# The first attention rounds of a fused sparse-attention and mixture-of-experts kernel: another order of their steps, unread matmuls beside them

## The chip, the core and the metric

The kernel runs on one core of a Trainium2 chip. The metric is device time in microseconds, the median of three runs. Five engines work side by side and wait for one another by semaphores: TensorE (PE: matmuls; PEld: its weight loads), VectorE (DVE), ScalarE (ACT), GpSimd (POOL) and SyncE (SP), which here issues the DMAs. Each engine takes its instructions in program order.

## The reference

Attention over 4 batches, 8 heads, 576 positions and 64 channels: heads 0 to 3 see the last 32 positions (local), heads 4 to 7 every 32nd position (strided). Its output, laid out as 2304 rows of 512, goes through 8 experts with a Sinkhorn gate.

```python
scores = scale * np.matmul(q, k.transpose(0, 1, 3, 2))
scores = np.where(masks[None], scores, -1e9)
attn = np.exp(scores - scores.max(-1, keepdims=True))
attn = attn / (attn.sum(-1, keepdims=True) + 1e-9)
x = np.matmul(attn, v).transpose(0, 2, 1, 3).reshape(2304, 512)
P = np.exp(x @ w_gate - max)          # then 8 x: rows to 1, columns to N / E
for e in range(8):
    out += P[:, e:e + 1] * (np.maximum(x @ w1[e], 0) @ w2[e])
```

## The kernel before

**Numbers.** To keep fp32 precision at the speed of the one-pass type, an operand is split into a high part (rounded, by ACT) and a low part (the rest, by DVE or POOL); a product is then three matmuls. This holds for x, the hidden layer h and the expert weights. Scores, transposes and values use plain fp32.

**Attention steps.** There are 32 steps k, eight for each batch: a pair of heads and half of the positions. In the order of `STEPS`, steps 0 to 3 of a batch are strided (0 and 2 with two blocks of 126 positions for each head, 1 and 3 with three blocks of 108), 4 to 7 local (4 and 5 with four windows, 6 and 7 with five). One step passes through all the engines:

- `at_scores`: PE multiplies queries and keys (tiles `sc`, L223 or L240), DVE scales and masks each window into `sm` and takes its extreme (L253), ACT takes the exponential and its sum (L259).
- `at_normalize`: DVE inverts the sums (L268, L269), POOL multiplies `sm` by them (L271).
- `at_transpose`: PE transposes `sm` into `tp` (L283), DVE copies it to `pt` (L284).
- `at_values`: PE multiplies with the values into `pv` (L296 or L310); ACT writes the high part of x into `reg` (L329), DVE the low part (L330). A strided step of the first batch does this in two pieces, and the second piece of ACT waits for the first of DVE.

`load_qkv(k)` issues two DMAs on SP: queries with keys (`qk`, three buffers) and values (`v`, five buffers). A load into a used buffer waits on SP until the matmuls that read it are done, and everything behind it on SP waits too.

**Weights.** Expert 0 is computed without a Strassen scheme, while attention is still running. Its weight tiles come in the order of the list `plain` by `load_w` into four slots of `raws`; `split_w` splits one (ACT L180, POOL L181) and issues the load of the next, which waits for POOL to have freed a slot. Before, `plain` alternates w1 and w2 tiles.

**Rounds.** Nine rounds k = 0 to 8 open the program, with LAG = 3: scores of k, values of k - 3, loads of k + 2, transposes of k - 2, normalization of k - 1, then one weight tile is split. Rounds 6 to 8 also begin the first layer of expert 0 (`begin_layer1`, L410: three matmuls for a weight tile ft and a quarter dt of the 512 channels; x of quarter dt must be there). Eight of the 16 pieces (ft, dt) are begun there, dt 2 and 3; the first four calls of `layer1` add dt 0 and 1.

**Slots.** Then come 56 slots. A slot has one call of `layer1` (tile `ph`, L424: 12 matmuls; h by ACT L430 and DVE L431) and the call of `layer2` of the slot before (tile `y`, L448: 6 matmuls). The first 26 also carry attention: layer1, values of k - 3, scores of k, layer2, transposes of k - 2, normalization of k - 1. After them the gate, the Strassen operands and the experts 1 to 7 follow; nothing of that changes.

PSUM tiles: tag s (scores), t (transposes; `pv` in the slots), y (`pv` in the rounds; `y`), l1 (`ph`), two buffers each.

Of the kernel before, what the change touches and what calls it, by code (L numbers as in the profile page):

```python
# [55 lines left out]
def kernel(  # L56
# [97 lines left out]
    plain = [(u, ft, which) for u in range(UPE) for ft in range(FH) for which in range(2)]  # L154
    plain[2 * FH :] = sorted(plain[2 * FH :], key=lambda x: (x[0], x[1] + 1.5 * x[2]))
# [43 lines left out]
    qkv_t, sms, sums_t, pts = {}, {}, {}, {}  # L199
# [87 lines left out]
    def at_values(k, tag):  # L287
# [40 lines left out]
        for src, (hi, lo) in moves:  # L328
            nc.scalar.activation(hi, src, AF.Copy)  # L329
            nc.vector.tensor_tensor(lo, src, hi.bitcast(F32), op=ALU.subtract)  # L330
# [84 lines left out]
    def layer1(u, c, ft):  # L415
        c0, n = c
        if u == 0 and c0 == 0:
            ph, dts = begun[ft // 2][:, ft % 2, :], (0, 1)
        else:
            ph, dts = ps.tile([P, 4 * P], F32, tag="l1", name=f"ph_{u}_{c0}_{ft}"), range(NDT)  # L420
        w = wt[u, ft, 0]
        for dt in dts:
            for i, x in ((0, 0), (0, 1), (1, 0)):
                nc.tensor.matmul(  # L424
                    ph[:, :n], w[:, i, dt, :], xv(x, dt, c0, n),
                    start=(dt + i + x == 0 and len(dts) == NDT),
                    stop=(dt == dts[-1] and i == 1), skip_group_check=len(dts) < NDT,
                )
        h = pools["h"].tile([P, 2, 4 * P], F32R, tag="h", name=f"h_{u}_{c0}_{ft}")
        nc.scalar.activation(h[:, 0, :n], ph[:, :n], AF.Relu)  # L430
        nc.vector.scalar_tensor_tensor(  # L431
            h[:, 1, :n], ph[:, :n], 0.0, h[:, 0, :n].bitcast(F32), op0=ALU.max, op1=ALU.subtract
        )
        hs[u, c0, ft] = h
# [553 lines left out]
    LAG = 3  # L988
    at_k = 0

    def attention_scores():
        if at_k < NS:
            at_scores(at_k)

    def attention_rest():


        nonlocal at_k
        if 0 <= at_k - 2 < NS:
            at_transpose(at_k - 2)  # L1000
        if 0 <= at_k - 1 < NS:
            at_normalize(at_k - 1)
        at_k += 1

    def attention_values(tag="t"):
        if at_k:
            store_x()
        if 0 <= at_k - LAG < NS:
            at_values(at_k - LAG, tag)
        if at_k:  # L1010
            load_qkv(at_k + 2)

    load_qkv(0)
    nc.sync.dma_start(cst, consts)
    load_qkv(1)
    load_qkv(2)
    for _ in range(4):
        load_w()
    nc.sync.dma_start(wg_raw, wg.rearrange("(k p) e -> p k e", p=P))
    nc.gpsimd.memset(ones, 1.0)  # L1020
    nc.gpsimd.memset(wgs.bitcast(F32), 0.0)
    for k in range(2 * NP - 2 + LAG):
        attention_scores()
        attention_values("y")
        attention_rest()
        if 1 <= k <= 2 * FH:
            split_w(*plain[k - 1])
        for x in {6: ((0, 2), (1, 2)), 7: ((2, 2), (0, 3)), 8: ((1, 3), (2, 3), (3, 2), (3, 3))}.get(k, ()):
            begin_layer1(*x)
    for dt in range(NDT):  # L1030
        c = 2 * E * dt
        nc.scalar.activation(wgs[:, c : c + E], wg_raw[:, dt, :], AF.Copy)
        nc.vector.tensor_tensor(
            wgs[:, c + E : c + 2 * E], wg_raw[:, dt, :], wgs[:, c : c + E].bitcast(F32),
            op=ALU.subtract,
        )
# [55 lines left out]
    for slot, (u, c, ft, last) in enumerate(slots):  # L1092
# [3 lines left out]
        busy = at_k < NS + LAG  # L1096
        if busy:
            attention_values()
# [8 lines left out]
        if busy:  # L1107
            attention_rest()
# [129 lines left out]
```

## Time and profile before

| | us |
|---|---|
| median of three runs | 1571.06 (1570.34 to 1572.72) |
| the profiled execution | 1571.07 |
| its span, first to last instruction | 1569.2 |
| PE busy in the span | 1550.7 (99%) |
| DVE, POOL, ACT busy | 1270.9, 972.0, 538.4 |
| HBM traffic | 413.82 MB, 264 GB/s |

A busy PE is not a PE at its peak: matmuls are pipelined and their ends are modelled. To see what bounds a stretch, the chain of waits is read: it goes back from the last instruction, at each step to what released it, or to the instruction before it on its engine. PE holds 94% of it.

### The profile page before, as it was taken

The numbers are of one execution on the slowest core, as the hardware profiler recorded it, in microseconds if no ns is written. First come the engines' busy times: TensorE is split into PE (matmuls) and PEld (weight loads), VectorE is DVE, ScalarE is ACT, GpSimd is POOL, SyncE is SP. The second block draws the span as 40 slices with busy tenths as digits, with TensorE's granted clock in tenths as the row PEclk, the third lists the DMA queues.
The fourth block names the chain that finished last, engine by engine and source line by source line (L and its number), as shares of the span: only waits on it lengthen the run. The fifth ranks groups of instructions, "written<-read, shape, count | busy, mean of one in ns | idle before, by whom it ended". The sixth has DMA issues, their size and how long they took to land.

```text
span 1569.2 us, 25435 instructions
## 1 busy us (share of the span) xinstructions
PE 1550.7 (99%) x9146; PEld 1455.8 (93%) x9146; DVE 1270.9 (81%) x2457; ACT 538.4 (34%) x1261; POOL 972.0 (62%) x899
## 2 busy tenths in 40 slices
PE   7999999999999999999999999999999999999999
PEld 5888887889999989898999999999999999999998
DVE  4665256689999999997688888888868888888887
ACT  6665222333434434342423322222232322222221
POOL 4222357265556565561777777877867777777874
PEclk9999999999999999999999999999999999999999
DMA  6553558897988888887967766766757666666762
GB/s 206 197 168 115 181 203 294 283 334 279 364 309 335 308 334 312 319 315 278 353 254 288 281 234 256 292 236 250 282 214 294 272 259 268 273 243 256 281 235 94
DMA packets 116622, 413.82 MB, mean 264 GB/s; under 512 B 9264, under 2 KB 63120, under 8 KB 102544
## 3 DMA queue, kind: packets, MB, share of 16 engines
q1 hardware_dynamic: 116496, 412.19, 69.7%
q8 instruction: 73, 1.20, 0.3%
q14 instruction: 53, 0.43, 0.1%
HBM read 275.27 MB, written 136.89 MB: 263 GB/s over the span
## 4 chain that ended last, share of the span: by engine, by line
PE 94%; DMA 2%; DVE 2%; POOL 1%; ACT 1%; issue 0%; SPq 0%; POOLq 0%; DVEq 0%; ACTq 0%
PE p L818 25%; PE bb L688 16%; PE yg L717 16%; PE bc L688 11%; PE ba L688 11%; PE y L448 6%; PE ph L424 5%; PE tp L283 1%; DMA rb<-in_w 1%; PE pv L296 1%; PE sc L223 1%; PE sc L240 1%; PE pv L310 1%; DMA qk<-in_qkv 1%; PE pl L339 1%; DMA sx<-xd 1%
## 5 line engine op out<-in xcount | busy, mean ns | idle before, releaser
L826 DVE TENSOR_TENSOR total<-p,total 128x384 f32<-128x384 f32 x714 | 371.9, 557 | 0.8 <-PE p L818 0.8
L688 PE MATMUL bb<-reg 128*128 128x384 f32 x1512 | 304.3, 335 | 1.1 <-DVE u L741 0.7
L688 PEld LDWEIGHTS bb<-reg 128*128 128x128 f32 x1512 | 266.0, 188 | 4.1 <-DVE u L741 1.0
L688 PE MATMUL bc<-reg 128*128 128x384 f32 x1008 | 201.9, 334 | 0.5 <-ACT h L749 0.5
L688 PE MATMUL ba<-reg 128*128 128x384 f32 x1008 | 201.8, 334 | 0.0
L799 ACT ACTIVATE a<-u 128x384 fp32r<-128x384 f32 x106 | 55.7, 525 | 359.3 <-DVE u L793 359.1
L741 DVE TENSOR_TENSOR u<-bb,m 128x384 f32<-128x384 f32 x168 | 93.3, 555 | 104.8 <-PE bb L688 101.5
L688 PEld LDWEIGHTS bc<-reg 128*128 128x128 f32 x1008 | 177.3, 188 | 0.8 <-ACT h L749 0.8
L688 PEld LDWEIGHTS ba<-reg 128*128 128x128 f32 x1008 | 177.3, 188 | 0.1
L875 POOL TENSOR_TENSOR s1t<-m,u 128x384 f32<-128x384 f32 x53 | 53.9, 1016 | 188.3 <-DVE m L793 188.3
L724 DVE SCALAR_TENSOR_TENSOR acc<-yg,gate,acc 128x512 f32<-128x512 f32 x186 | 131.4, 741 | 9.6 <-PE yg L717 9.6
L717 PE MATMUL yg<-w2b,h 128*128 128x512 f32 x504 | 117.4, 390 | 0.4 <-DVE acc L724 0.4
L717 PE MATMUL yg<-w2t,h 128*128 128x512 f32 x504 | 117.1, 390 | 0.0
L818 PE MATMUL p<-s,w2b 128*128 128x384 f32 x648 | 116.7, 334 | 0.0
L717 PEld LDWEIGHTS yg<-w2b,h 128*128 128x128 f32 x504 | 94.3, 188 | 20.0 <-DVE acc L724 0.9
L448 PE MATMUL y<-w2t,h 128*128 128x512 f32 x432 | 111.4, 399 | 1.3 <-DVE acc L461 0.9
L818 PEld LDWEIGHTS p<-s,w2b 128*128 128x128 f32 x648 | 112.7, 188 | 0.0
L818 PE MATMUL p<-s,w2t 128*128 128x384 f32 x624 | 112.3, 334 | 0.0
L717 PEld LDWEIGHTS yg<-w2t,h 128*128 128x128 f32 x504 | 94.4, 188 | 19.1
L424 PE MATMUL ph<-reg,w 128*128 128x256 f32 (+1 forms) x648 | 110.4, 319 | 0.0
L803 POOL TENSOR_TENSOR a<-u,a 128x384 fp32r<-128x384 f32 x106 | 109.4, 1032 | 0.0
L818 PEld LDWEIGHTS p<-s,w2t 128*128 128x128 f32 x624 | 108.5, 188 | 0.0
(149 smaller groups left out, 2865.1 us busy)
## 6 DMA issues: line engine op xcount, KB each, us to landing
reg<-wd SPq DMA_DIRECT2D x52, 1792.0 KB
wd<-reg SPq DMA_DIRECT2D x28, 1792.0 KB
w2b<-w2d SPq DMA_DIRECT2D x25, 1792.0 KB
w2t<-w2d SPq DMA_DIRECT2D x24, 1792.0 KB
w2d<-w2b SPq DMA_DIRECT2D x14, 2048.0 KB
w2d<-w2t SPq DMA_DIRECT2D x14, 2048.0 KB
raws<-in_w SPq DMA_DIRECT2D x72, 256.0 KB
sx<-xd SPq DMA_DIRECT2D x24, 384.0 KB
```

The source lines that it names most:

```text
L223: nc.tensor.matmul(scs[i % 2][o : o + QT, i // 2, :], t[sl, q0 : q0 + QT], t[sl, k0 : k0 + KW], start=True, stop=True,)
L424: nc.tensor.matmul(ph[:, :n], w[:, i, dt, :], xv(x, dt, c0, n), start=(dt + i + x == 0 and len(dts) == NDT), stop=(dt == dts[-1] and i == ...
L448: nc.tensor.matmul(y, h[:, a, i * P : (i + 1) * P], w[:, b, :], start=(ft == 0 and first), stop=(ft == FH - 1 and a == 1),)
L688: nc.tensor.matmul(out[:, :TN], w[:, i, k, :], xops[x][:, xi, k, :], start=(start and n == 0), stop=(n == 5), skip_group_check=True,)
L717: nc.tensor.matmul(y, hg[g, i // 3, f][:, a, o : o + P], w[:, b, f, :], start=(f == 0 and a + b == 0), stop=(f == 1 and a == 1),)
L724: nc.vector.scalar_tensor_tensor(acc[:, i, :], y, gate[:, t, e : e + 1], acc[:, i, :], op0=ALU.mult, op1=ALU.add)
L741: nc.vector.tensor_tensor(o, bank[:, :TN], s, op=ALU.add)
L799: nc.scalar.activation(t[:, 0], src, AF.Copy)
L803: nc.gpsimd.tensor_tensor(t[:, 1], src, t[:, 0].bitcast(F32), op=ALU.subtract)
L818: nc.tensor.matmul(y[:, :TN], w[:, b, wi, d, :], h[:, a, :], start=(a + b == 0), stop=(a == 1),)
L826: nc.vector.tensor_tensor(o, y[:, :TN], o, op=ALU.add)
L875: nc.gpsimd.tensor_tensor(s1, m1, u3, op=ALU.add)
```

## The change

1. **The unread matmuls.** `keep_busy(n)` issues n matmuls of the zeroed tile `wgs` (128 rows, 128 weight columns, 192 columns) into a PSUM tile `spare` of tag y that nobody reads: 14 ahead of the first scores, 6 behind those of round 0, 4 behind those of rounds 1 to 5. `wgs` is zeroed first on POOL; its real content, the split gate weights, moves to slot 2 (`split_gate`) and its load behind the rounds.
2. **The rounds.** Eight instead of nine, and LAG 2. In a round: loads of k + 2, high part of x of k - 3 (`x_high`), transposes of k - 2, normalization of k - 1, scores of k, low part of x of k - 3 (`x_low`), the unread matmuls, begun pieces of layer 1, values of k - 2, one weight split. The last round takes its scores behind its values. The high and the low part no longer alternate: ACT writes both pieces, then DVE.
3. **The slots.** In an attention slot: layer1, loads, scores of k, transposes of k - 2, layer2, normalization of k - 1, values of k - 2, both parts of x. So the values stand behind the transposes of their own step in the same slot. Their number stays 26.
4. **Weights and loads.** `plain` has the four w1 tiles first; 12 pieces of layer 1 are begun instead of 8, and the first four calls of `layer1` add 3 matmuls instead of 6; `layer1` takes its quarters in the order 2, 3, 0, 1. The first half of the constants is loaded on ACT's queue; two weight tiles are loaded ahead of the rounds, two more in rounds 1 and 2; the eighth split stands in slot 0.

In the order of instructions, names read as follows: the first number behind `sc`, `sm`, `tp`, `pt` is the head of the pair, in `ph` the first column and ft, in `y` the first column and the tile; the last number is a running one. On PE, the beginning of the program before, up to the first transposes:

```order
L240 MATMUL sc_0_135<-qk_115 126x126 x2
L240 MATMUL sc_1_136<-qk_115 126x126 x2
L240 MATMUL sc_0_154<-qk_120 108x108 x3
L240 MATMUL sc_1_155<-qk_120 108x108 x3
L240 MATMUL sc_0_191<-qk_124 126x126 x2
L240 MATMUL sc_1_192<-qk_124 126x126 x2
L283 MATMUL tp_0_0_215<-cst,sm_0_142 126x126 x2
L283 MATMUL tp_1_0_220<-cst,sm_1_148 126x126 x2
```

And now:

```order
L1029 MATMUL spare_-1_133<-wgs 128x192 x14
L241 MATMUL sc_0_148<-qk_116 126x126 x2
L241 MATMUL sc_1_149<-qk_116 126x126 x2
L1029 MATMUL spare_167<-wgs 128x192 x6
L241 MATMUL sc_0_183<-qk_120 108x108 x3
L241 MATMUL sc_1_184<-qk_120 108x108 x3
L1029 MATMUL spare_208<-wgs 128x192 x4
L284 MATMUL tp_0_0_223<-cst,sm_0_155 126x126 x2
L284 MATMUL tp_1_0_228<-cst,sm_1_161 126x126 x2
L241 MATMUL sc_0_236<-qk_125 126x126 x2
```

The transposes of step 0 moved ahead of the scores of step 2, and unread matmuls stand behind each step's scores. On ACT, rounds 3 and 4 before (exponentials of steps 3 and 4, x of steps 0 and 1):

```order
L259 ACTIVATE sm_0_240,sums_239<-sm_0_240,mx_0_241 108x108 x3
L259 ACTIVATE sm_1_248,sums_239<-sm_1_248,mx_1_249 108x108 x3
L329 ACTIVATE reg<-pv_256 128x16x14
L329 ACTIVATE reg<-pv_256 128x2x14
L180 ACTIVATE w_0_1_285<-raws 128x512
L259 ACTIVATE sm_0_300,sums_299<-sm_0_300,mx_0_301 128x96 x4
L329 ACTIVATE reg<-pv_310 128x16x18
L329 ACTIVATE reg<-pv_310 128x2x18
```

And now:

```order
L333 ACTIVATE reg<-pv_260 128x16x14
L333 ACTIVATE reg<-pv_260 128x2x14
L260 ACTIVATE sm_0_300,sums_299<-sm_0_300,mx_0_301 108x108 x3
L260 ACTIVATE sm_1_308,sums_299<-sm_1_308,mx_1_309 108x108 x3
L181 ACTIVATE w_0_2_330<-raws 128x512
L333 ACTIVATE reg<-pv_323 128x16x18
L333 ACTIVATE reg<-pv_323 128x2x18
L260 ACTIVATE sm_0_365,sums_364<-sm_0_365,mx_0_366 128x96 x4
```

The high part of x of step 0 stands ahead of the exponentials of step 3 instead of behind them. On PE, a slot of the later stretch before (layer 1 of ft 3, chunk 256; values of step 13, scores of step 16, layer 2, transposes of step 14):

```order
L424 MATMUL ph_256_3_1076<-reg,w_0_3_505 128x256 x12
L296 MATMUL pv_1092<-pt_0_1066,v_743 64x64 x8
L240 MATMUL sc_0_1107<-qk_957 126x126
L240 MATMUL sc_1_1108<-qk_957 126x126
L240 MATMUL sc_0_1107<-qk_957 126x126
L240 MATMUL sc_1_1108<-qk_957 126x126
L448 MATMUL y_256_0_986<-w2t,h_256_2_1017 128x512 x3
L448 MATMUL y_256_1_987<-w2t,h_256_2_1017 128x512 x3
L283 MATMUL tp_0_0_1133<-cst,sm_0_974 96x128 x4
L283 MATMUL tp_0_4_1139<-cst,sm_0_974 96x128
```

And a slot now (ft 2, chunk 512; scores and transposes, layer 2, then the values of the step just transposed):

```order
L432 MATMUL ph_512_2_1314<-reg,w_0_2_330 128x256 x12
L241 MATMUL sc_0_1335<-qk_1173 126x126
L241 MATMUL sc_1_1336<-qk_1173 126x126
L241 MATMUL sc_0_1335<-qk_1173 126x126
L241 MATMUL sc_1_1336<-qk_1173 126x126
L284 MATMUL tp_0_0_1355<-cst,sm_0_1184 126x126 x2
L284 MATMUL tp_1_0_1360<-cst,sm_1_1190 126x126 x2
L456 MATMUL y_512_0_1287<-w2t,h_512_1_1245 128x512 x3
L456 MATMUL y_512_1_1288<-w2t,h_512_1_1245 128x512 x3
L311 MATMUL pv_1374<-pt_0_1354,v_1031 64x126
L311 MATMUL pv_1374<-pt_1_1359,v_1031 64x126
```

The values moved from behind layer 1 to the end of the slot, behind one layer 2 after their transposes.

The diff, without what repeats the text above:

```diff
@@ -152,6 +152,7 @@
 
 
     plain = [(u, ft, which) for u in range(UPE) for ft in range(FH) for which in range(2)]
+    plain[: 2 * FH] = sorted(plain[: 2 * FH], key=lambda x: x[2])
     plain[2 * FH :] = sorted(plain[2 * FH :], key=lambda x: (x[0], x[1] + 1.5 * x[2]))
     raw = {}
     wt = {}
...
@@ -325,8 +326,15 @@
                 )
                 for t, m in pieces(b * S, S)
             ]
-        for src, (hi, lo) in moves:
+        moved[k] = moves
+
+    def x_high(k):
+        for src, (hi, _) in moved[k]:
             nc.scalar.activation(hi, src, AF.Copy)
+
+    def x_low(k):
+        b = steps[k][0]
+        for src, (hi, lo) in moved.pop(k):
             nc.vector.tensor_tensor(lo, src, hi.bitcast(F32), op=ALU.subtract)
         if k % len(STEPS) == len(STEPS) - 1:
             done.extend(c for c in range(NC) if b * S < min(NT, (c + 1) * CH) <= (b + 1) * S)
@@ -415,15 +423,15 @@
     def layer1(u, c, ft):
         c0, n = c
         if u == 0 and c0 == 0:
-            ph, dts = begun[ft // 2][:, ft % 2, :], (0, 1)
-        else:
-            ph, dts = ps.tile([P, 4 * P], F32, tag="l1", name=f"ph_{u}_{c0}_{ft}"), range(NDT)
+            ph, dts = begun[ft // 2][:, ft % 2, :], (1,)
+        else:
+            ph, dts = ps.tile([P, 4 * P], F32, tag="l1", name=f"ph_{u}_{c0}_{ft}"), (2, 3, 0, 1)
         w = wt[u, ft, 0]
         for dt in dts:
             for i, x in ((0, 0), (0, 1), (1, 0)):
                 nc.tensor.matmul(
                     ph[:, :n], w[:, i, dt, :], xv(x, dt, c0, n),
-                    start=(dt + i + x == 0 and len(dts) == NDT),
+                    start=(dt == 2 and i + x == 0),
                     stop=(dt == dts[-1] and i == 1), skip_group_check=len(dts) < NDT,
                 )
         h = pools["h"].tile([P, 2, 4 * P], F32R, tag="h", name=f"h_{u}_{c0}_{ft}")
@@ -985,55 +993,88 @@
             next(w2n, None)
 
 
-    LAG = 3
-    at_k = 0
+    LAG = 2
 
     def attention_scores():
+        store_x()
+        load_qkv(at_k + 2)
         if at_k < NS:
             at_scores(at_k)
-
-    def attention_rest():
-
+        at_transpose(at_k - 2)
+
+    def attention_values():
 
         nonlocal at_k
-        if 0 <= at_k - 2 < NS:
-            at_transpose(at_k - 2)
-        if 0 <= at_k - 1 < NS:
+        if at_k - 1 < NS:
             at_normalize(at_k - 1)
+        at_values(at_k - 2, "t")
+        x_high(at_k - 2)
+        x_low(at_k - 2)
         at_k += 1
 
-    def attention_values(tag="t"):
-        if at_k:
-            store_x()
-        if 0 <= at_k - LAG < NS:
-            at_values(at_k - LAG, tag)
+    WARM = 2 * NP - 1
+    nc.scalar.dma_start(cst[:, :2], consts[:, :2])
+    load_qkv(0)
+    load_qkv(1)
+    load_w()
+    load_qkv(2)
+    load_w()
+    nc.sync.dma_start(cst[:, 2:], consts[:, 2:])
+    nc.gpsimd.memset(wgs.bitcast(F32), 0.0)
+    nc.gpsimd.memset(ones, 1.0)
+
+    def keep_busy(n):
+        spare = ps.tile([P, 4 * P], F32, tag="y", name=f"spare_{at_k}")
+        for _ in range(n):
+            nc.tensor.matmul(
+                spare[:, : wgs.shape[1]], wgs[:, :P], wgs, start=True, stop=True
+            )
+
+    at_k = -1
+    keep_busy(14)
+    ahead = {
+        5: ((0, 2), (1, 2)), 6: ((2, 2), (3, 2), (0, 3), (1, 3)),
+        7: ((2, 3), (3, 3), (0, 0), (1, 0), (2, 0), (3, 0)),
+    }
+    for at_k in range(WARM + 1):
+        last = at_k == WARM
         if at_k:
             load_qkv(at_k + 2)
-
-    load_qkv(0)
-    nc.sync.dma_start(cst, consts)
-    load_qkv(1)
-    load_qkv(2)
-    for _ in range(4):
-        load_w()
+        if 1 <= at_k <= 2:
+            load_w()
+        if at_k >= 3:
+            x_high(at_k - 3)
+        if at_k >= 2:
+            at_transpose(at_k - 2)
+        if at_k >= 1:
+            at_normalize(at_k - 1)
+        if not last:
+            at_scores(at_k)
+        if at_k >= 3:
+            x_low(at_k - 3)
+        if at_k < 6:
+            keep_busy(6 if at_k == 0 else 4)
+        for x in ahead.get(at_k, ()):
+            begin_layer1(*x)
+        if at_k >= 2:
+            at_values(at_k - 2, "y")
+        if last:
+            x_high(at_k - 2)
+            x_low(at_k - 2)
+            at_scores(at_k)
+        if at_k:
+            split_w(*plain[at_k - 1])
+    at_k = WARM + 1
     nc.sync.dma_start(wg_raw, wg.rearrange("(k p) e -> p k e", p=P))
-    nc.gpsimd.memset(ones, 1.0)
-    nc.gpsimd.memset(wgs.bitcast(F32), 0.0)
-    for k in range(2 * NP - 2 + LAG):
-        attention_scores()
-        attention_values("y")
-        attention_rest()
-        if 1 <= k <= 2 * FH:
-            split_w(*plain[k - 1])
-        for x in {6: ((0, 2), (1, 2)), 7: ((2, 2), (0, 3)), 8: ((1, 3), (2, 3), (3, 2), (3, 3))}.get(k, ()):
-            begin_layer1(*x)
-    for dt in range(NDT):
-        c = 2 * E * dt
-        nc.scalar.activation(wgs[:, c : c + E], wg_raw[:, dt, :], AF.Copy)
-        nc.vector.tensor_tensor(
-            wgs[:, c + E : c + 2 * E], wg_raw[:, dt, :], wgs[:, c : c + E].bitcast(F32),
-            op=ALU.subtract,
-        )
+
+    def split_gate():
+        for dt in range(NDT):
+            c = 2 * E * dt
+            nc.scalar.activation(wgs[:, c : c + E], wg_raw[:, dt, :], AF.Copy)
+            nc.vector.tensor_tensor(
+                wgs[:, c + E : c + 2 * E], wg_raw[:, dt, :], wgs[:, c : c + E].bitcast(F32),
+                op=ALU.subtract,
+            )
...
@@ -1094,8 +1135,11 @@
         if last and u + 1 < UPE:
             split_w(u + 1, ft, 0)
         busy = at_k < NS + LAG
+        if slot == 0:
+            split_w(*plain[WARM])
+        elif slot == 2:
+            split_gate()
         if busy:
-            attention_values()
             attention_scores()
         if slot == len(slots) - 1:
             rest = [(prev[:3], None), ((u, c, ft), None)]
@@ -1105,7 +1149,7 @@
             if plast and pu + 1 < UPE:
                 split_w(pu + 1, pft, 1)
         if busy:
-            attention_rest()
+            attention_values()
             if at_k == NS + LAG:
                 store_x()
                 open_pools("right", ("sb", 1))
```

## Rows read from the trace of the kernel before

**Rows 1.** Two stretches: length, busy us of PE, PEld, DVE, ACT, POOL, clock, DMA, GB/s.

```profile
0.00:45.00 45.00, 33.65 (x318) 26.96 (x318) 23.27 (x145) 27.72 (x122) 19.36 (x27) 1.00 0.63 202
45.00:160.00 115.00, 115.00 (x1207) 98.64 (x1202) 69.62 (x365) 69.01 (x291) 26.33 (x36) 1.00 0.48 157
```

**Rows 2.** Timeline of PE: start, us, line, shapes, idle before and its releaser.

```profile
3.48 1.22 PE L240 MATMUL sc<-qk 64*126 64x126 f32 x8 [3.48 <-DMA qk<-in_qkv]
...
29.45 1.63 PE L410 MATMUL ph<-reg,w 128*128 128x256 f32 x6
...
33.51 0.96 PE L410 MATMUL ph<-reg,w 128*128 128x256 f32 x6
...
36.05 0.69 PE L296 MATMUL pv<-pt,v 96*64 96x64 f32 x16 [0.94 <-DVE pt L284]
```

**Rows 3.** The chain of waits, 1 to 28 us: start, us, what held it.

```profile
1.65 0.42 SPq L1014
...
2.12 4.63 DMA qk<-in_qkv
...
6.89 1.40 PE sc L240 x9
...
8.62 2.32 ACT sm L259 x12
10.94 0.53 ACT w L180
...
13.13 1.41 POOL sm L271 x2
...
20.31 1.24 POOL w L181
...
22.00 4.14 DMA qk<-in_qkv
```

**Rows 4.** The chain of waits, 32 to 52 us.

```profile
32.77 1.91 ACT sm L259 x10
34.68 0.28 ACT reg L329
...
34.98 0.42 DVE reg L330
35.40 0.59 DVE pt L284
...
36.10 0.20 DVE sums L269
...
38.26 1.43 PE ph L410 x12
...
40.40 0.73 PE pv L296 x20
41.13 0.75 PE sc L240 x12
...
45.13 0.64 PE sc L240 x8
45.77 1.59 PE y L448 x6
...
47.78 0.71 PE ph L424 x6
...
51.41 0.56 PE tp L283 x6
```

**Rows 5.** Timeline of ACT and DVE in one slot, 86 to 90 us.

```profile
86.30 0.38 ACT L430 ACTIVATE h<-ph 128x256 fp32r<-128x256 f32 x1 [0.75 <-PE ph L424]
86.72 0.43 DVE L431 SCALAR_TENSOR_TENSOR h<-ph,h 128x256 fp32r<-128x256 f32 x1 [1.06 <-ACT h L430]
...
88.93 0.27 DVE L253 CUSTOM_DVE_ANT_0 sm<-sc,cst 108x108 f32<-108x108 f32 x1
...
89.44 0.90 DVE L284 COPY pt<-tp 108x324 f32<-108x324 f32 x2 [0.24 <-PE tp L283]
```

More of the change, by code (lines that the diff above doesn't have):

```diff
@@ L198 @@
     QK = -(-max(sum(_columns(*x)[:2]) for x in STEPS) // P) * P
-    qkv_t, sms, sums_t, pts = {}, {}, {}, {}
+    qkv_t, sms, sums_t, pts, moved = {}, {}, {}, {}, {}
     def load_qkv(k):
```

## The prediction, made before the changed kernel ran

> **What bounds the kernel now.** First the busy time by stretches [rows 1]: from 45 to 160 us PE is busy all 115.00 of 115.00 us, in the first 45 us only 33.65, so 11.35 us of PE idle time lie ahead of the slots. Behind 160 us the change moves nothing, and PE hardly waits there (1550.7 us busy of a span of 1569.2): a slot that comes earlier brings the end forward by nearly as much. The question is when the first layer 2 (`y`) starts, at 45.77 [rows 4], and whether the new slots stay gapless.
>
> The second view is PE's timeline [rows 2]. The same six matmuls of L410 take 1.63 us at 29.45 and 0.96 at 33.51. Other shapes agree: the twelve scores of a 108 step hold the chain for most of 1.40 us at 6.89 [rows 3] and 0.75 at 41.13 [rows 4]. [...] What came ahead of the rise was PE work without a pause that held the first full-size matmuls; a pause of 0.94 us later did not undo it [rows 2].
>
> [...]
>
> The third view is the chain of waits [rows 3, 4]. It shows a loop through all engines: scores, extremes, exponential (2.32 or 1.91), a weight split (0.53 on ACT, 1.24 on POOL), normalization 1.41, transposes, copy, extremes again. PE holds less than half of it. Twice a DMA holds it: the queries of step 1 (to 6.75) and those of step 6, which wait on SP until POOL has freed a weight slot (21.55) and land 4.6 us later, at 26.14 [rows 3].
>
> **The change part by part.**
>
> *Unread matmuls.* Forty of 192 columns. Six matmuls of 256 columns take 0.71 us at full speed [rows 4] and 1.63 at half [rows 2], so one costs 0.09 to 0.12, or 0.20 to 0.27. The first 14 (at most 3.8 us) start when POOL has zeroed `wgs`, at about 1 us, and PE has nothing else until 3.48 [rows 2]; 0 to 0.4 us stick out, and the first scores' masks come later anyway, so nothing is taken. The other 26 cost 2.3 to 3.1 us at full speed, 5.2 to 7 at half. Their cover is PE's idle 11.35 us: a round's PE work at full speed (transposes 0.56, scores 0.75, values 0.73, spares 0.4) is 2.4 us against 3 to 4.7 of the loop. Taken: 0, if the clock is full. Their worth is that the clock rises at about 4 to 8 us instead of 32.
>
> *The loop to the first `y`,* laid end to end from the rows. The constants leave SP's queue (an issue of 0.42 with 0.05 around it), so the queries of step 1 land at 6.3 instead of 6.75 [rows 3]. The scores with their first extremes took 1.73 us to the exponential; at full speed I take 1.25 (1.0 to 1.4): exponential 1 at 7.7, done 10.0. Split on ACT 0.53, on POOL 1.24: 11.8. The first half of normalization 0.7, transposes 0.56, copy 0.59, extremes about 0.9: exponential 3 at 14.5, done 16.8. Split 0.53 and 1.24: POOL frees the slot at 18.6 instead of 21.55. SP still loads a weight tile and then step 6 behind that wait, 4.6 us: 23.2. This wait stays; it only moves. Scores 0.64 and an extreme: exponential 6 at 24.25, done 26.15; split 0.53; high x twice 0.28: 27.3; copy 0.59 and extremes 0.4: 28.3; low x 0.42; twelve begun matmuls 1.43: 30.2; values 0.73: 30.9; high x 0.28, low 0.42, extremes: exponential 7 at 32.05, done 33.95; split 0.53; h 0.38 and 0.43: 35.3; extremes 0.9; copy 0.59; values 0.73: 37.5; layer 1 0.36, scores 0.75, transposes 0.56 and a wait of 0.3: first `y` at **39.5**, against 45.77 [rows 4], 6.3 us earlier.
>
> *Work not yet done there.* Before, scores (0.64) and values (0.73) of one more step stood ahead of that point, now six more matmuls of layer 1 (0.71): 0.66 goes off the gain. The number of begun and later pieces of layer 1 does not change their sum. The end of the ping-pong between ACT and DVE is in the chain above. The gate's split and load are small and have a slot of time; the split of the eighth tile in slot 0 is 0.53 on ACT, which is idle 40% of the slots [rows 1]. I cost them at nothing.
>
> *The slots.* Values now stand one layer 2 behind their transposes. From the end of layer 1: h high 0.09 + 0.38, h low 0.43, then DVE is free at +0.97 [rows 5]; six extremes at a spacing of 0.19 bring it to +2.1, a copy of `pt` of 0.45 (half of 0.90, both heads) twice to +3.1. PE reaches the values at +0.75 + 0.56 + 1.59 = +2.89. So a slot with two 108 steps may wait 0.2; with other shapes the four or five extremes leave 0 to 0.1. Before, a copy had a whole slot. There are about three slots of the worst kind, and the first slots have their DVE work late: I take 0.9 us in sum, between 0 and 26 times 0.3 = 8.
>
> *Sum.* 6.3 − 0.66 − 0.9 = 4.7 us.
>
> **The rivals.** *The clock rises late or falls back (R1).* Between bursts of a round PE still waits 1 to 2 us; before, only 0.94 was survived [rows 2]. At half speed a round's transposes and scores (1.3) take as long again, about half of it on the chain: 0.7 a round. Full only from round 5 on costs 2.8: gain 1.9, 1569.2 us. For it speaks that the first six matmuls of a round are small; against it the 14 ahead, 2 to 3 us without a pause.
> [...]
>
> *The clock stays at half until the full-size work of rounds 5 to 7 (R2), slower.* Then the spares cost 0.8 a round at half speed, a round's PE work grows to 4.4 to 5 us and becomes the chain: seven rounds at 0.7, and in three of them the spares' 0.8 besides, 7.3 against 4.7: 1573.7. It decides at about 25 us: a rise later than that makes the change a loss. For it: the same little matmuls never raised it before 29 us. This is also the case that the spares do not do what they are there for.
>
> *The copies wait in every slot (R3), slower.* If DVE or ACT is later than reckoned, the wait stands in all 26 slots, since PE has no other work between layer 2 and the values. At 0.2 each it is 5.2, gain 0.4: 1570.7; at 0.3 it is 7.8 and the time 1573.5; at 0.4, 1576. It decides at 0.22 a slot (5.6 over 26). For it: the margin of a 108 slot is already negative. Against it: DVE is busy 69.62 of 115 us [rows 1].
>
> *The constants on ACT's queue delay the first queries:* at most 0.5 us, inside the range.
>
> **How the numbers follow.** The profiled execution took 1571.07, the median is 1571.06: no correction. 1571.07 − 4.7 = **1566.4 us**. The forecast's own case (waits of 0.5 to 1.3 less or more, clock full between 4 and 12 us): 1564.5 to 1567.9, chance 0.57; better still 0.03. R1 0.20 (1567.9 to 1571), R2 0.07, R3 0.13. A measurement of this kernel tells 0.2% (3.1 us) from no change: faster is below 1567.9, 0.60; R1 and the milder half of R2 and R3 lie within it, 0.31; the rest of R2 and R3 is slower, 0.09. The range leaves out 0.03 below and the greater part of R2 and R3 above: 1564.5 to 1572.0.
>
> **What would show it.** In the profile after: scores of 108 steps at about 0.8 us from round 1 on instead of 1.4 to 1.9 (else R1 or R2); exponential 6 at about 24.3, first `y` at about 39.5; layer 1 of the slots at half speed nowhere. PE busy from 45 to 160 us at least 114 of 115; a group of values released by the copy of `pt` with 5 us of idle time would be R3. The wait of SP for POOL at 18.6 and the landing of step 6 at 23.2 are the step that I trust least: a weight load that lands later shifts all behind it one for one.

## The result and the profile after

The changed kernel takes 1580.73 us (median of six runs, 1579.90 to 1581.58) against 1570.76 for the kernel before in the same runs: a ratio of 1.0064, 95% interval 1.0051 to 1.0076. It is 10 us slower; 4.7 us faster was forecast. The profiled execution took 1579.90 with a span of 1578.0.

Two stretches of the changed kernel, with the columns of [rows 1]:

```profile
0.00:45.00 45.00, 39.30 (x327) 32.43 (x327) 20.66 (x124) 24.81 (x106) 19.49 (x26) 0.98 0.58 187
45.00:160.00 115.00, 114.98 (x1154) 93.50 (x1154) 65.42 (x375) 66.58 (x298) 25.43 (x35) 0.98 0.49 161
```

PE is busier in the opening than before (39.30 us for 33.65) and as busy as before in the slots, yet it does less there: 1154 matmuls from 45 to 160 us for 1207. Busy time doesn't show what is lost, the lengths of single pieces do. The timeline of PE:

```profile
1.05 3.31 PE L1029 MATMUL spare_-1_133<-wgs 128*128 128x192 f32 x14 [1.05 <-POOL wgs L1023]
...
15.29 1.91 PE L241 MATMUL sc<-qk 64*108 64x108 f32 x12
...
25.88 0.69 PE L1029 MATMUL spare<-wgs 128*128 128x192 f32 x4
26.41 0.91 PE L418 MATMUL ph<-reg,w 128*128 128x256 f32 x6
...
31.46 0.86 PE L418 MATMUL ph<-reg,w 128*128 128x256 f32 x5 [1.20 <-DVE reg L338]
...
42.87 1.34 PE L297 MATMUL pv<-pt,v 96*64 96x64 f32 x20 [2.53 <-DVE pt L285]
...
47.38 2.70 PE L456 MATMUL y<-w2t,h 128*128 128x512 f32 x6
50.02 0.80 PE L297 MATMUL pv<-pt,v 96*64 96x64 f32 x20
...
52.34 1.64 PE L456 MATMUL y<-w2t,h 128*128 128x512 f32 x6
```

Up to 25.8 us everything is at half speed (scores of a 108 step 1.91 at 15.29, and 0.82 at 55.27; the unread matmuls 0.213 us from start to start, and 0.11 behind 25.9), though PE hardly paused from 1.05 on. Six matmuls of L418 at 26.41 take 0.91 us, much as those of [rows 2] at 33.51 (0.96). PE comes through a wait of 1.20 us at 31.46 at full speed. Then it waits 2.53 us for the copy of step 6 in slot 0, and behind that wait it is at half speed again: the same values take 1.34 at 42.87 and 0.80 at 50.02. Here the granted clock shows it too (stretches of five us, columns of [rows 1]; the clock is the third figure from the right):

```profile
35.00:40.00 5.00, 4.75 (x62) 3.95 (x63) 1.31 (x11) 2.13 (x11) 0.69 (x1) 1.00 0.48 158
40.00:45.00 5.00, 2.47 (x27) 1.96 (x24) 2.70 (x14) 3.60 (x15) 3.48 (x3) 0.79 0.27 65
45.00:50.00 5.00, 5.00 (x24) 3.86 (x23) 3.05 (x19) 2.70 (x13) 0.87 (x2) 0.53 0.69 230
50.00:55.00 5.00, 5.00 (x52) 3.90 (x52) 2.97 (x19) 3.08 (x16) 0.73 (x2) 1.00 0.39 153
```

The changes of the granted clock in the trace stand at 25.82 (1.00, called full here), 42.89 (0.50, half) and 49.71 (1.00). Nothing is recorded ahead of the first change, and the view then reads 1.00: that is why [rows 1] shows 1.00 also where the scores of a 108 step take 1.88 us in the kernel before (at 6.89; 0.82 at 41.06, behind its rise at 32.8).

The chain of waits through the rounds shows the unread matmuls themselves:

```profile
5.51 1.52 PE spare L1029 x6
7.03 1.84 PE sc L241 x12
8.87 1.10 PE spare L1029 x4
9.96 0.84 PE tp L284 x4
10.80 1.16 PE sc L241 x8
11.96 1.10 PE spare L1029 x4
...
17.19 1.11 PE spare L1029 x4
...
21.58 1.11 PE spare L1029 x4
...
25.95 0.62 PE spare L1029 x4
```

Six bursts, 6.6 us. In [rows 3] the chain went through ACT, POOL and the DMAs here; now it is PE.

The third loss is in the slots. The eight slots of a batch, from one layer 2 to the one eight slots later, before and (second fence) after:

```profile
53.88 1.65 PE L448 MATMUL y<-w2t,h 128*128 128x512 f32 x6
...
92.25 1.68 PE L448 MATMUL y<-w2t,h 128*128 128x512 f32 x6
```

```profile
61.77 1.64 PE L456 MATMUL y<-w2t,h 128*128 128x512 f32 x6
...
101.55 1.64 PE L456 MATMUL y<-w2t,h 128*128 128x512 f32 x6
```

38.37 us before, 39.78 now, with the same work, no pause shown and the clock full: 0.175 us a slot.

**Where the time went.** The first layer 2 starts at 47.38 instead of 45.70 in PE's timeline (the chain, from which [rows 4] has 45.77, splits neighbours a little differently). From there to the gate's first matmul it is 122.27 us (to 169.65) instead of 116.07 (to 161.77). So 1.7 us are lost ahead of it, 6.2 in the slots (0.66 of that is the work that stands there now), and 0.9 behind the gate, where nothing was changed. From the gate's first matmul to the end it is 1407.4 us before and 1408.4 after, and 1406.6 to 1409.8 in the traces of the runs below, without a pattern; so nothing is read into it, and the whole times of two single executions can't be compared to better than some 3 us.

### The profile page after: what moved, and what is told of

Read it like the earlier page. It is cut to its first block, busy times and chain, and to the rows that moved or that the text cites. A ratio compares the mean times of both kernels' runs of the same rounds, so it can differ in the third digit from the quotient of the medians.

```text
span 1578.0 us, 25538 instructions
## 1 busy us (share of the span) xinstructions
PE 1564.4 (99%) x9186; PEld 1462.8 (93%) x9186; DVE 1267.4 (80%) x2457; ACT 536.0 (34%) x1261; POOL 971.9 (62%) x899
## 4 chain that ended last, share of the span: by engine, by line
PE 92%; DVE 3%; DMA 2%; POOL 1%; ACT 1%; issue 0%; SPq 0%; DVEq 0%; ACTq 0%; POOLq 0%
PE p L826 24%; PE bb L696 16%; PE yg L725 16%; PE ba L696 11%; PE bc L696 11%; PE ph L432 5%; PE y L456 4%; PE tp L284 1%; DMA sx<-xd 1%; PE sc L241 1%; DMA w2t<-w2d 1%; PE pv L311 1%; PE pv L297 1%; POOL sx L547 1%; PE sc L224 1%; PE pl L347 1%
```

## The experiments

Theories on the opening: the unread matmuls cost and warm nothing (A), or they did bring the clock's rise forward (B); products of zeros don't count (C), or the data is nothing to it (D); what ran was too small (H), or the kind doesn't matter (I). On the slots: values wait for their copy (E), or there is one change more between matmuls whose first shape in the timeline has a 64, here called half (values `96*64`, scores `64*108`), and those in which both figures are more, called full (layers `128*128`, transposes `108*108`) (F). On the seam: the pause let the clock fall (J), or not (K). All in one table (us; rise and fall of the clock and starts from each trace; "8 slots" as above; the ratio is to the kernel before in the same runs):

| run | median | ratio, 95% | rise | fall to rise | first layer 2 | 8 slots |
|---|---|---|---|---|---|---|
| before | 1570.8 | | 32.8 | none | 45.70 | 38.37 |
| after | 1580.73 | 1.0051 to 1.0076 | 25.8 | 42.9 to 49.7 | 47.38 | 39.78 |
| e1_no_spares | 1577.31 | 1.0025 to 1.0055 | 25.2 | 38.8 to 45.7 | 44.90 | 39.76 |
| e2_spares_of_ones | 1580.29 | 1.0043 to 1.0073 | 28.2 | 41.8 to 48.7 | 47.91 | 39.74 |
| e3_values_later | 1579.29 | 1.0038 to 1.0071 | 28.1 | 45.1 to 52.0 | 49.47 | 39.54 |
| e4_scores_last | 1577.21 | 1.0028 to 1.0058 | 30.4 | 44.0 to 47.5 | 47.30 | 38.64 |
| e5_wide_ahead | 1581.81 | one run | 6.6 | 20.3 to 30.5, 44.2 to 51.0 | 50.35 | 39.77 |
| e6_before_y_between | 1576.52 | 1.0021 to 1.0047 | 31.1 | none | 44.32 | 39.70 |
| e7_seam | 1578.93 | 1.0032 to 1.0060 | 30.5 | none | 45.17 | 39.75 |
| e8_best | 1571.79 | 0.9993 to 1.0010 | 18.2 | 21.6 to 28.5 | 41.64 | 38.65 |
| e9_after_wide | 1577.69 | 1.0034 to 1.0062 | 6.0 | 16.3 to 19.7, 40.2 to 47.0 | 44.86 | 39.77 |
| e10_before_wide | 1570.03 | 0.9988 to 1.0006 | 6.4 | none | 43.95 | 38.40 |
| e11_best_wide | 1570.24 | 0.9985 to 1.0003 | 5.0 | 15.2 to 22.0 | 40.88 | 38.65 |
| e12_best_wide6 | 1571.97 | 0.9998 to 1.0017 | 4.9 | 39.0 to 42.5 | 40.64 | 38.64 |

**Without the unread matmuls.**

```diff
-    keep_busy(14)
...
-        if at_k < 6:
-            keep_busy(6 if at_k == 0 else 4)
```

> The changed kernel without its 40 unread matmuls; all else as in it. In the changed kernel TensorE ran at half speed until 25.8 us although it never paused from 1.05 us on, the 26 unread matmuls of the rounds held 6.6 us of the chain up to there, and the first layer 2 began at 47.7. Theory A (they cost and warm nothing): the chain loses them, the clock rises no earlier than 25.8 and no later than about 32, first layer 2 at 43 to 45, time 1576.5 to 1578.5. Rival B (they brought the rise forward from 32.8 to 25.8): without them it rises at 32 or later, first layer 2 at 48 or later, time 1581 to 1584.

The median falls by 3.4 us and the clock rises at 25.2, no later than with them. Theory A had 25.8 at the earliest and fits in all else. The forty matmuls were a loss.

**Ones instead of zeros.**

```diff
-    nc.gpsimd.memset(wgs.bitcast(F32), 0.0)
+    nc.gpsimd.memset(wgs.bitcast(F32), 1.0)
...
+        nc.gpsimd.memset(wgs.bitcast(F32), 0.0)
```

> The unread matmuls multiply a tile of ones in place of zeros (it is zeroed in slot 2, ahead of its real content); all else as in the changed kernel. Theory C (products of zeros count for nothing with the clock gate): the rise comes between 4 and 12 us, first layer 2 at 40 to 42, time 1573 to 1575. Rival D (the data doesn't matter): rise at 24 to 27 us, time within 0.1% of the changed kernel, 1579 to 1582.

Rise at 28.2, a little outside D's 24 to 27, and the same time as the changed kernel: theory D, as far as constants go; varied data was not tried.

**Values one step later at the same place in the slot.**

```diff
-    LAG = 2
+    LAG = 3
...
-        at_values(at_k - 2, "t")
-        x_high(at_k - 2)
-        x_low(at_k - 2)
+        at_values(at_k - 3, "t")
+        x_high(at_k - 3)
+        x_low(at_k - 3)
...
```

> The slots of the changed kernel keep their order of shapes, but the values that stand behind layer 2 are those of the step before, whose copy was done a slot earlier; one more round (scores of step 8, transposes of step 6) stands ahead of the slots for it. Between the last start of layer 2 and the first of the values the changed kernel has 0.328 us on average (0.317 to 0.411), before it was 0.230 from layer 2 to the transposes. Theory E (values wait for the copy): the gap falls to 0.23 or less and a slot gets 0.1 to 0.2 shorter. Rival F (one more change between full tiles of the array and half ones in each slot, four for three, at about 0.09 each): the gap stays at 0.31 to 0.33, only the extra 0.08 in slots with 108 x 108 values goes, and a slot gets shorter by 0.03 or less. The time itself moves by the extra round too: 1576 to 1579 by E, 1579 to 1583 by F.

From the last start in layer 2 to the first in the values it is 0.325 us on average over 19 slots (0.328 in the changed kernel), though the copy had been done a slot earlier. Eight slots get 0.24 shorter, 0.03 a slot, and 0.195 of that is one wait inside the values in the slot of two 108 steps (from their first to their last start 0.715 in the changed kernel, where the other slot of 108 values has 0.520, as here and before). Theory F; the wait for the copy was only a sixth of the loss.

**Scores at the end of the slot, beside the values.**

```diff
     def attention_scores():
...
-        if at_k < NS:
-            at_scores(at_k)
+        while exps:
+            exps.pop(0)()
         at_transpose(at_k - 2)
...
         x_low(at_k - 2)
+        if at_k < NS:
+            at_scores(at_k, exps)
```

> The slots of the changed kernel in the order layer 1, transposes of k - 2, layer 2, values of k - 2, scores of k; the exponentials of the scores are issued in the next slot behind its h. Values and scores stand side by side, so that there are three changes between full and half tiles in a slot again instead of four. Theory F: a slot gets 0.10 to 0.17 shorter, 26 of them 2.6 to 4.4 us, time 1576 to 1578. Rival E (the values' wait for the copy): the copy has no extremes ahead of it now, so it gains as well, but the gap from layer 2 to the values falls to 0.23; by F it stays at 0.32. Rival G (exponentials come too late for the transposes of the slot after the next): transposes wait for normalization, time above 1582.

Eight slots take 38.64 us, 0.14 a slot less, and the median falls by 3.5. The gap between layer 2 and the values stays at 0.325, as F said: what went is another change. A slot and its neighbours in the timeline of PE:

```profile
90.26 1.63 PE L462 MATMUL y<-w2t,h 128*128 128x512 f32 x6
91.82 0.65 PE L317 MATMUL pv<-pt,v 126*64 126x126 f32 x8
92.41 0.71 PE L241 MATMUL sc<-qk 64*126 64x126 f32 x8
93.04 1.70 PE L438 MATMUL ph<-reg,w 128*128 128x256 f32 x12
94.58 0.74 PE L290 MATMUL tp<-cst,sm 108*108 108x108 f32 x6
95.09 1.64 PE L462 MATMUL y<-w2t,h 128*128 128x512 f32 x6
```

Layer 1 to transposes takes 1.54 from start to start here, and 1.62 from layer 1 to scores in the changed kernel.

**The kernel before, with layer 2 between values and scores.**

```diff
         if busy:
             attention_values()
-            attention_scores()
...
             layer2(pu, pc, pft)
...
         if busy:
+            attention_scores()
             attention_rest()
```

> The kernel before with one thing changed: in each of the attention slots layer 2 stands between the values and the scores (layer 1, values, layer 2, scores, transposes), which makes four changes between full and half tiles in a slot out of three. Same work, same rounds, same waits. Theory F (about 0.09 for a change, 0.05 more for the first transposes behind half tiles): 24 slots at 0.10 to 0.17, time 1573.0 to 1574.8. Rival E (only waits cost): 1570 to 1571.5.

Only the order of the same matmuls in the slot is other, and the kernel is 5.3 us slower. Eight slots take 39.70 us, 0.17 a slot more, with 0.324 between layer 2 and the scores. The direction is F's. The size is above its range (1573.0 to 1574.8): 24 slots at 0.17 are 4.0, and the waits were not the same, as the values of the second and third slot now also wait for the copy, 0.16 and 0.48 us ahead of them and 0.3 inside each, 1.3 in sum. (Of the 0.17, 0.02 are such waits in slots of two 108 steps.) This shows the slots' loss in a kernel whose opening was never touched.

**The seam.**

The end of the last round (the two splits move to the slots):

```diff
-            at_scores(at_k)
-        if at_k:
+            at_scores(at_k, exps)
+            at_transpose(at_k - 1)
+        elif at_k:
             split_w(*plain[at_k - 1])
```

> The changed kernel with another seam between rounds and slots: transposes and copy of step 6 stand at the end of the last round, h of slot 0 ahead of the exponentials of step 7, and the two weight splits of round 7 and slot 0 behind the x of slots 0 and 1. In the changed kernel TensorE waited 2.53 us for that copy, and when it went on the granted clock was 0.50 for 6.83 us. Theory J (the pause let the clock fall): the pause gets shorter than 1.2 us, the clock doesn't fall, first layer 2 at 42 to 44 instead of 47.4, time 1575 to 1577.5. Rival K (the fall has another cause, or the pause only moves to the transposes of step 7): the clock falls again between 38 and 48 us, time 1578.5 to 1581.

The longest pause at the seam is now 0.91 us, and the clock doesn't fall: that part of J holds. The time lies outside J's range and in that of K, though K's fall of the clock didn't come: the rise came at 30.5 in this execution, 4.7 us later than in the changed kernel's profile, and behind the first layer 2 there are new waits. Pauses of PE there:

```profile
44.12 0.64 PE L290 MATMUL tp<-cst,sm 128*96 128x128 f32 x4 [0.91 <-POOL sm L278]
...
47.42 0.80 PE L303 MATMUL pv<-pt,v 96*64 96x64 f32 x20 [0.64 <-DVE pt L291]
...
52.13 0.97 PE L317 MATMUL pv<-pt,v 126*64 126x126 f32 x8 [0.75 <-DVE pt L291]
...
60.02 0.56 PE L224 MATMUL sc<-qk 64*64 64x96 f32 x16 [0.77 <-DMA qk<-in_qkv]
```

In the profiled execution the first layer 2 is 2.2 us earlier than in the changed kernel and the gate's first matmul 0.9; the median is 1.8 lower, with runs from 1576.1 to 1580.4, so the gain of the seam by itself is not clear of the noise.

**Wide unread matmuls ahead.**

```diff
-    keep_busy(14)
+    keep_busy(24, wide)
...
```

`wide` is a zeroed tile of 512 columns, the second operand of these 24.

> The changed kernel, but ahead of the first scores stand 24 unread matmuls of 512 columns instead of 14 of 192; they push the first scores back to about 11 us, so the time itself says little. So far the rise of the clock came at 25 to 31 us in five kernels, with and without unread matmuls of 192 columns, with zeros and with ones. Theory H (what ran before the rise is too small, not too short): the clock rises while the wide ones run or just behind them, before 14 us, and the time is then 1577 to 1581 although the first scores start 7 us later. Rival I (the kind of matmul doesn't matter): the rise comes behind 20 us as before, and the time is 1584 to 1589.

The clock rises at 6.6 us, within the wide ones, for the first time. The stretches show also how it was lost again:

```profile
5.00:10.00 5.00, 5.00 (x25) 3.82 (x23) 0.00 (x0) 0.00 (x0) 0.00 (x0) 1.00 0.71 230
...
15.00:20.00 5.00, 3.33 (x35) 2.48 (x31) 2.62 (x15) 3.19 (x14) 3.89 (x5) 1.00 0.43 154
20.00:25.00 5.00, 4.94 (x40) 3.86 (x40) 3.40 (x19) 3.22 (x15) 2.63 (x4) 0.53 0.55 157
25.00:30.00 5.00, 4.94 (x38) 3.90 (x38) 3.96 (x23) 3.20 (x16) 3.29 (x4) 0.50 0.58 200
```

PE paused 1.47 us at 16.3 and 0.20 at 18.3 between small matmuls, and from 20.3 on it was at half speed, though it then hardly paused. First scores start 5.3 us later than in the changed kernel, and the one run is 1.1 slower, 0.8 above H's range; the rise, by which H was to be told, is H's.

**Wide ones at the places of the narrow ones.**

```diff
-    keep_busy(14)
+    keep_busy(8)
...
-            keep_busy(6 if at_k == 0 else 4)
+            keep_busy(3)
...
```

> The changed kernel with other unread matmuls at the same places: 512 columns of zeros in place of 192, 8 ahead of the first scores and 3 behind the scores of rounds 0 to 5. With 24 of them ahead the clock had risen at 6.6 us, and fallen at 20.25 behind pauses of 0.7 and 1.5 us and rounds with small matmuls. Theory H (the wide ones raise it and hold it): rise at 5 to 10 us, held to the seam, first layer 2 between 41 and 44 instead of 47.4, the fall at the seam as before, time 1575 to 1578. Rival L (the pauses of the rounds bring it down all the same): rise by 10 us, fall between 12 and 30, time 1579 to 1582.

Rise at 6.0, one fall of 3.4 us from 16.3 on: in the rounds between H and L. The first layer 2 is 2.5 us earlier than in the changed kernel, the median 3.0; the fall at the seam (2.53 us pause again) stays. But e1, with no unread matmuls and at half speed up to 25.2, has the same: 44.90 for 44.86, and 1577.31 for 1577.69. So the clock was up in nearly all rounds, and with the matmuls that brought it up on board nothing was gained over leaving all of them out.

**The same in the kernel before.**

```diff
...
+    keep_busy(8)
     for k in range(2 * NP - 2 + LAG):
         attention_scores()
+        if k < 6:
+            keep_busy(3)
         attention_values("y")
```

> The kernel before, nothing moved, with unread matmuls of 512 columns of zeros: 8 ahead of the first scores, 3 behind the scores of rounds 0 to 5, into the tag of layer 1, which is free until round 6. Theory H: rise at 5 to 10 us instead of 31 to 33, PE's part of each round at half the length, first layer 2 at 41 to 44 instead of 45.7, time 1567 to 1570. Rival M (the rounds hang on ACT, DVE, POOL and the DMA of step 6, so that an earlier clock gives little): 1570 to 1572. Rival L (the clock falls in the rounds and the wide ones then cost 1.3 us a round): 1572 to 1576.

The rise is at 6.4 and it holds through pauses of up to 1.08 us. Half of the gain in the first layer 2 (1.75 us) is left in the median at most: 0.8 us, an interval that holds no change. Theory M is as near as H. What PE waits for in the rounds at full speed:

```profile
12.52 1.07 PE L240 MATMUL sc<-qk 64*108 64x108 f32 x12 [1.08 <-DMA qk<-in_qkv]
...
23.24 0.49 PE L283 MATMUL tp<-cst,sm 108*108 108x108 f32 x3 [0.56 <-POOL sm L271]
...
30.46 0.69 PE L296 MATMUL pv<-pt,v 96*64 96x64 f32 x16 [0.96 <-DVE pt L284]
```

**All mended parts together:** the slots of e4 and the seam of e7, without unread matmuls (e8), with 8 wide ones ahead and 3 in each of the first six rounds (e11), and with more of them in the rounds (e12). From e11 to e12:

```diff
         if at_k < 6:
-            keep_busy(3)
+            keep_busy((3, 4, 6, 6, 6, 3)[at_k])
```

> No unread matmuls, the slots of the run with the scores last, and the new seam together; rounds as in the changed kernel. If the three parts add up (3.4 without the unread matmuls, 3.5 for the order of the slots, 3 to 6 for the seam, from 1580.7): 1568 to 1571, so at best 0.15% faster than the kernel before. Rival (the pause at the seam comes back, as scores and exponentials stand later in the slots): 1573 to 1577.

> The run with the new seam and the scores last in the slots (1571.8, first layer 2 at 41.6, clock full from 18.2 and again half from 21.6 to 28.5), with the wide unread matmuls of 512 columns: 8 ahead, 3 behind the scores of rounds 0 to 5. Theory H: rise at 5 to 10 us and no fall, first layer 2 at 38.5 to 40.5, time 1568 to 1570.5. Rival L: the clock falls in between, time 1571 to 1574.

> As the last run (new seam, scores last in the slots, 8 wide unread matmuls ahead), but behind the scores of rounds 0 to 5 stand 3, 4, 6, 6, 6 and 3 of them instead of 3 each. In the last run the clock was half from 15.2 to 22.0 us, behind a pause of 1.20 us at 13.4 and shorter ones; three more of them take 0.96 us. Theory J (pauses bring it down): the pauses ahead of round 4 stay under 0.6 us, the clock holds from the rise on, first layer 2 at 39.5 to 40.5 instead of 40.9, time 1568.5 to 1570, at best 0.1% under the kernel before. Rival N (more of them delay the values behind them by as much as the clock gives): 1570 to 1572.

The medians are 1571.8, 1570.2 and 1572.0, none of which can be told from the kernel before, nor clearly from one another. e8 misses its range of 1568 to 1571 since the seam gave less than was put in: with its measured 1.8 the parts add up (1572.0). e11 has the fall of L and the time of H, e12 the time of N. In e12 the clock is full from 4.9 to 39.0 us, in e8 it is half from the first scores (4.1) to 18.2 and from 21.6 to 28.5, 21 us of the same rounds; the first layer 2 starts at 40.64 and 41.64. One us is left of it, or two, if the later first scores of e12 (5.1) are counted. That isn't the worth of the clock alone, since the wide ones stand in the chain of e12 at full speed too, here 2.5 us of it:

```profile
15.59 1.58 PE spare L1041 x6
...
22.84 0.89 PE spare L1041 x3
```

J's word on the pauses is borne out up to round 7; then e12 falls too, at 39.0, inside the second of two pauses of 0.75 and 1.19 at the seam, and the layer 2 that was to gain is the one that runs slowly:

```profile
36.51 0.80 PE L303 MATMUL pv<-pt,v 96*64 96x64 f32 x20 [0.75 <-DVE pt L291]
...
39.69 1.30 PE L290 MATMUL tp<-cst,sm 128*96 128x128 f32 x5 [1.19 <-POOL sm L278]
40.64 2.47 PE L462 MATMUL y<-w2t,h 128*128 128x512 f32 x6
```

In e8 the same instructions have the same two pauses and the clock holds (so it does in e11, with 0.75 and 1.19):

```profile
37.96 0.80 PE L303 MATMUL pv<-pt,v 96*64 96x64 f32 x20 [0.75 <-DVE pt L291]
...
41.13 0.75 PE L290 MATMUL tp<-cst,sm 128*96 128x128 f32 x5 [1.18 <-POOL sm L278]
41.64 1.64 PE L462 MATMUL y<-w2t,h 128*128 128x512 f32 x6
```

## Why the prediction was wrong, step by step

The profiled execution is 13.5 us above the forecast: 7.9 up to the first layer 2 (47.4 for 39.5), 4.6 in the slots (5.5 for 0.9), 0.9 behind them. Of the 7.9, 2.7 are there at exponential 3 (17.16 for 14.5), 6.2 at exponentials 6 and 7 (30.44 for 24.25, 38.25 for 32.05), and the last 1.7 come behind that.

**"Their worth is that the clock rises at about 4 to 8 us instead of 32": failed.** It rose at 25.8, and in e1 without them at 25.2. That 14 matmuls without a pause would do it, by 4 to 8 us, was a guess that no run shows: with 512 columns the clock rose at 4.9 to 6.6, with these 192 at 25.8 to 30.5 (after, e2 to e4, e7). The rows had a rise only behind the first full-size layer 1 work, and rival R2 was built on just that ("the same little matmuls never raised it"). It had a chance of 0.07 and should have had the greater one. Its tie to the full-size work isn't borne out either: the rise came 0.6 us ahead of the first of it in the changed kernel, and 5 us ahead in e8 (18.2 for 23.3). With the wide ones of e5 and e9 to e12 it did rise early.

**"Taken: 0, if the clock is full": the condition failed, and with it the cover.** At half speed (the last four at full) the 26 matmuls behind the scores took 6.6 us of the chain, inside the 5.2 to 7 that were given for half speed. Without them the median is 3.4 lower. That full speed would have covered them isn't shown: in e12 2.5 us of the wide ones stand in the chain at full speed.

**The loop, laid end to end: another path, and mis-sized.** From exponential 3 to exponential 6 the forecast has 9.75 us, by way of POOL's split, SP and the queries of step 6. In the changed kernel they start at 17.16 and 30.44 (13.3 us, 4.4 a round); the chain there is PE at half speed up to the rise, as R2 had it (4.4 to 5), and no DMA is in it between them, nor in e1 and e12. In the other traces:

```profile
16.06 0.39 ACT L260 ACTIVATE sm<-sm,mx 108x108 f32<-108x108 f32 x1 [2.35 <-DVE mx L254]
...
27.96 0.37 ACT L260 ACTIVATE sm<-sm,mx 128x96 f32<-128x96 f32 x1 [1.54 <-DVE mx L254]
```

That is e1 (11.9 us): the new order without unread matmuls, at half speed up to 25.2. It is 11.7 in e12 (15.77 to 27.45), the new order at full speed with wide ones; 13.5 before (14.53 to 28.03), the old order at half speed; 12.9 in e10 (13.77 to 26.66), the old order at full speed. So the new order is quicker by 1.6 us at half speed and by 1.2 at full, where 3.75 was forecast, and the clock gives 0.6 in the old order. In two of the rounds of e12's chain the copy, the inversion of the sums and the extremes pass through DVE one behind the other. What the new order takes at full speed without unread matmuls in its chain no run shows; how much of the 9.75 was out of reach stays open.

**"Layer 1 0.36, scores 0.75, transposes 0.56 and a wait of 0.3": the pause was there, what follows it was not.** The long wait of PE in slot 0 was in the chain, hidden in the sum of ACT's and DVE's terms. That PE stands still for 2.53 us meanwhile and comes out of it at half speed (granted 0.50 from 42.89 to 49.71) is rival R1's mechanism at another place (I had put it in the rounds). From exponential 7 to the first layer 2 it took 9.1 us instead of 7.45.

**The slots, 0.9 us: wrong cause and a fifth of the size.** Of the 5.5 us, 1.2 are the half speed up to 49.7; 4.3 are the slots' own. R3 put the danger at the right place, between layer 2 and the values, and at 0.2 us a slot; the measured 0.175 is near it. But its mechanism, the wait for the copy, makes up 0.02 to 0.03 (e3). (R3's 1573.5 for 0.3 a slot should read 1573.2; nothing hangs on it.) The rest is the order of the shapes. Means over the slots, from the starts of single matmuls in the traces: between the last of one group and the first of the next

| | before | after | e4 |
|---|---|---|---|
| layer 1 to what follows | 0.209 (values) | 0.209 (scores) | 0.120 (transposes) |
| layer 2 to what follows | 0.230 (transposes) | 0.328 (values) | 0.325 (values) |
| scores to what follows | 0.181 (layer 2) | 0.181 (transposes) | 0.180 (layer 1) |
| values to what follows | 0.174 (scores) | 0.174 (layer 1) | 0.173 (scores) |
| inside four transposes | 0.325 | 0.374 | 0.325 |

Values and scores have the half shapes (`96*64`, `64*108`), the other three the full ones. It isn't the number type: transposes are plain fp32 like values and scores, and stand 0.120 behind layer 1. Going from full to half costs about 0.09 to 0.10 here (0.209 for 0.120 behind layer 1, 0.328 for 0.230 behind layer 2), and the first transposes behind half ones 0.05. Before, values and scores were neighbours, so that a slot went from full to half once; now it does so twice, behind layer 1 and behind layer 2: 0.10 + 0.05 + 0.02 (layer 1, whose own twelve take 1.412 for 1.392) − 0.02 (layer 2) + 0.02 (108 steps) = 0.17. I priced the moved groups by their lengths and their waits, and the places between groups at nothing.

**Right:** PE stays gapless in the slots (114.98 of 115). The wait in slots of two 108 steps is there: 0.195 inside the values, where 0.2 was forecast. R2 had the mechanism of the opening's loss up to the rise. That its size fits too (2.3 us with the 0.66 of work, R2 had 2.6) is partly luck, since the fall at the seam is in it, and R2's limit of about 25 us for the rise isn't shown: e7 rose at 30.5 and e9 at 6.0, and their first layer 2 starts at 45.17 and 44.86.

## What to carry to other kernels

Price the places between groups of matmuls too: in a tuned loop keep those of half shapes next to each other, since one further change between half and full cost 0.14 to 0.17 us a slot here (e4, e6), and showed neither as idle time nor as a wait. Before matmuls are added to keep the clock up, test in a run of its own that this shape raises it and that no pause behind them takes it down again; where they fail they are work at half speed on the chain. And ask whether the time follows the clock: here it rose 13 to 26 us earlier with the wide ones, and none of the pairs with and without them (e9 and e1, e11 or e12 and e8, e10 and the kernel before) can be told apart by their medians.

## What the runs showed of the hardware that was not expected

The rise of the clock isn't fixed for a program: five kernels with the same opening up to the last round, but for the ones of e2 (after, e2 to e4 and e7), rose at 25.8, 28.2, 28.1, 30.4 and 30.5 us; e8, with the rounds of e1, rose at 18.2, with no unread and no full-size matmul ahead of it, and fell again at 21.6, where e1 rose at 25.2. An opening that hangs on it can only be compared over several runs. In the changed kernel TensorE hardly paused from 1.05 to 25.8 us, with 36 of its matmuls of 192 columns between scores, transposes and values, and stayed at half speed: four of them took 1.17 us at 21.51, as in e5 at 28.41, where the granted clock is 0.50. With eight of 512 columns from 1.5 us on and three or more in each of the first rounds the clock was full by 4.9 to 6.4 us (e9 to e12; three of them take 0.95 to 0.97 us between 5.7 and 6.4, and 1.65 at 15.76 in e11, at half). A fall came in or soon behind the long pause at the seam in all seven traces that have one (2.0 to 3.0 us: after, e1 to e5, e9), and behind or in pauses of 1.47 (e5), 1.45 (e8), 1.20 (e9, e11), and 0.75 with 1.19 (e12). But the changed kernel came through 1.20, e10 through 1.08, and e8 and e11 through the same 0.75 with 1.18 and 1.19. So with pauses of about a microsecond their length doesn't tell whether the clock falls, and what does was not found.
